# Rounding g behind its leaky step, another product order in the first batch, and another order at both ends of an attention + two-MoE kernel

## The chip, the cores and the metric

The kernel runs on one core of a Trainium2 chip. The metric is the device time of one execution in microseconds. The core has a matrix engine (TensorE, PE in the profile; its weight loads are PEld), VectorE (DVE), ScalarE (ACT), GpSimd (POOL), a sync engine (SP) that issues transfers, and 16 DMA engines. TensorE writes PSUM, which VectorE and ScalarE read; each engine works off its own queue in order.

## The reference, cut to what matters

```python
# q, k, v: (8, 8, 576, 64), phi: (8, 8, 576, 32)
a = exp(phi - max(phi, axis=2)); a = a / (sum(a, axis=2) + 1e-9)
k_m = einsum('bhsm,bhsd->bhmd', a, k); v_m = einsum('bhsm,bhsd->bhmd', a, v)
attn = softmax(q @ k_m^T / 8)            # over the 32 memory slots
x = (attn @ v_m), heads side by side     # (4608, 512)
h = x @ w_in; g = maximum(0.01 * h, h); x = g @ w_out                 # 512 -> 2048 -> 512
out = (sigmoid(x @ w_gate) * (x @ w_val)) @ w2_out                    # 512 -> 1536 -> 512
```

The inputs arrive as 64-bit floats and the output is 32-bit.

## The kernel before

The inputs are 64-bit numbers read as pairs of 32-bit words; ScalarE, VectorE and GpSimd turn each piece of a weight into a 32-bit float in steps called a, b, b2, c, d. A call of `tick` advances this pipeline by one piece. The wide products are made from numbers split into a rounded high part (a cast on ScalarE) and the rest (a subtraction on VectorE or GpSimd), three products for one: `split` does this.

**Stage one** goes over 8 batches of 576 tokens. A unit is (batch, group of 4 heads); its softmaxes run as a chain of small steps v1, t1, v2, ..., v11, where t steps are TensorE products and v steps work on the other engines. v_m is multiplied into w_in beforehand (`vw_block`, or `vw_pair` from batch 1 on), so that the hidden layer comes from the attention weights at_hi, at_lo directly. A loop step i stands for one half of a batch (288 tokens) and 128 of the 2048 hidden columns. `m1_in` makes the six hidden products into a bank of ps_h (two banks), Prelu (L861) puts the leaky result into grs, and the function that m1_in returns splits it into ghl (cast at L188, subtraction at L189). `m1_out` multiplies g into w_out: twelve products into four accumulators (L880); where a group of hidden columns ends, the accumulators are copied or added to obuf or pbuf (L887, L889). m1_in runs two steps ahead (LA = 2).

The order of the work is written out by hand. In step i of the loop (L1373 on) these are queued: the split of the g of step i + 1 (`fin`), the six products and the Prelu of step i + 2, the v steps of units due now together with ticks (or, later, the preparation of the second stage's weights, `stash`), the t steps, the v_m blocks, and last the output products of step i. The first batch (steps 0 to 31) runs while w_in and w_out are still being decoded; its order of halves is four hidden blocks for one half, four for the other. Ahead of the loop a prologue of groups (`SCHED['prologue']`) runs units (0,0) and (0,1); in a group the entries of one unit form a chain, T is a tick, and the chains take turns. Behind the prologue come v_m blocks 0 and 1 and m1_in for steps 0 and 1.

**Stage two** takes tokens in five pairs of blocks with seven products for eight, with the output products in `m2_out` (L1165), whose results VectorE adds into sums (L1175). In the last pair of 2 x 384 tokens the sums are turned by 32x32 transposes (L1147) into tiles called turned and stored (L1205): in chunks of 256 and 128 tokens, a transpose is put on a list (`lazy`) and runs behind later additions, and each store of four transfers goes out when all of the columns of one block of tokens are turned, in rows of 128 floats.

The lines in question:

```python
        gr = gr_next()
        nc.scalar.activation(gr, p[:, :HALF], AF.Prelu, alpha=0.01)
        gt[b, hf, fc] = (gh, gl)
        return lambda: split(gr, gh, gl, nc.vector if ... else nc.gpsimd)
```

Of the kernel before, what the change touches and what calls it, by code (L numbers as in the profile page):

```python
# [26 lines left out]
 'ticks': [1, 1, 1, 1, 2, 1, 1, 2, 0, 1, 0, 1, 1, 2, 0, 0, 0, 1, 1, 1, 1, 1, 0, 0, 1, 0, 0, 0, 0, 0],  # L27
 'banks': 9,
 'lopool': [0, 1, 2, 3, 4, 5, 6, 7, 8, 9, 10, 11, 12, 13, 14],
# [93 lines left out]
def tile_kernel(  # L123
# [13 lines left out]
    nc = tc.nc  # L137
# [274 lines left out]
    def ghl_next():  # L412
        n_g[1] += 1
        i = n_g[1] % 3
        return ghl[:, i, :], ghl[:, 3 + i, :]
# [426 lines left out]
    gt = {}  # L842
    acc = {}

    def m1_in(b, hf, fc):
        p = ps_h.tile([P, 512], F32, tag="h", name="ps_h")
        t = vw[b, fc * P // VB]
        o = (fc * P) % VB
        n = 0
        for g in range(NG):  # L850
            wh, wl = t[:, 0, g, o:o + P], t[:, 1, g, o:o + P]
            i = at[b, hf, g]
            ah, al = at_hi[:, i, :], at_lo[:, i, :]
            if fc == NF - 1:
                at_free.append(i)
            for w, x in ((wh, ah), (wl, ah), (wh, al)):
                nc.tensor.matmul(p[:, :HALF], w, x, start=(n == 0), stop=(n == 3 * NG - 1))  # L857
                n += 1
        gh, gl = ghl_next()
        gr = gr_next()  # L860
        nc.scalar.activation(gr, p[:, :HALF], AF.Prelu, alpha=0.01)  # L861
        gt[b, hf, fc] = (gh, gl)
        return lambda: split(gr, gh, gl, nc.vector if b == 0 and hf * NF + fc in SCHED["gldve"] else nc.gpsimd)
# [139 lines left out]
    def read(*todo, turns=0):  # L1003
        for op in todo:
            op()
        n_read[0] += 1
        for op in later.pop(n_read[0], []):
            op()
        for _ in range(turns):
            if lazy:  # L1010
                lazy.pop(0)()
# [129 lines left out]
    def m2_out(n, th, between):  # L1141
        t0, h = PAIRS[n]
        last = th == NTH - 1
        end = n + 1 == len(PAIRS)

        def turn(j, e, x, m, st):
            lazy.append(lambda: nc.vector.transpose(  # L1147
                st[:, 0:m // 32, j - j % 2 + e], sums[j][:, e, x:x + m].rearrange("p (b r) -> p b r", r=32),
            ))

        def stored(t, x, m, st):
            f = lazy.pop()
            lazy.append(lambda: (f(), store(t0 + t * h + x, m, st, end)))

        chunks = [(0, 256), (256, h - 256)]
        st = {}
        for k, e in OUT_SEQ:
            start = k in (0, 2, 3)
            b = banks[e if k in (0, 1, 4, 6) else 2 + e][:, :h]
            wt = w_at.pop(0)  # L1160
            w = wt.rearrange("p (j l f) -> p j l f", j=TH // 2, l=2)
            i = 0
            for j in range(TH // 2):
                for l, r in ((0, 0), (0, 1), (1, 0)):
                    nc.tensor.matmul(  # L1165
                        b, w[:, j, l, :], ops[j][k][:, r, :h], start=(start and i == 0), stop=(i == 5),
                        skip_group_check=not start,
                    )
                    i += 1
            w_load(wt)  # L1170
            o = sums[SUM_OF[k]][:, e, :h]
            if th == 0 and k in (0, 2, 1, 6):
                read(lambda: nc.scalar.copy(o, b), turns=1)
            else:
                read(lambda: nc.vector.tensor_add(o, b, o), turns=2 if end and last else 1)  # L1175
            for f in between.pop(0) if between else ():
                f()
            if last and end and (j := {5: 1, 4: 3, 3: 0, 6: 2}.get(k)) is not None:
                t = j % 2
                for x, m in chunks:  # L1180
                    if (t, x) not in st:
                        st[t, x] = turned()
                    turn(j, e, x, m, st[t, x])
                    if (k, e) in ((4, 1), (6, 1)):
                        stored(t, x, m, st[t, x])
            elif last and not end and (k, e) in ((4, 1), (6, 1)):
                t = k == 4
                for x, m in chunks:
                    o = turned()
                    for j in (t, t + 2):  # L1190
                        for e2 in range(2):
                            turn(j, e2, x, m, o)
                    stored(t, x, m, o)
        while last and end and lazy:
            lazy.pop(0)()

    n_st = [0]

    def turned():
        n_st[0] += 1  # L1200
        return stage2[n_st[0] % len(stage2)]

    def store(n0, m, o, end):
        for g in range(4):
            (nc.scalar if end and g % 2 else nc.sync).dma_start(  # L1205
                out=out[n0:n0 + m, P * g:P * g + P].rearrange("(b p) d -> p b d", p=32),
                in_=o[32 * g:32 * g + 32, 0:m // 32].rearrange("p b q r -> p b (q r)"),
            )


    with tc.manual_schedule():
# [84 lines left out]
        def step_in(b, hf, fc):  # L1296
            if (b, hf) == (0, 0):
                done_until(2 * (fc - fc % 2) + 4)
            return m1_in(b, hf, fc)
# [5 lines left out]
        def unit_parts(i):  # L1305
            vs, ts_, ls = [], [], []
            for u, u0 in U0.items():
                parts = [n for n, k in SCHED[{1: "chain1", 2: "chain2"}.get(u[0], "chain")].items() if k == i - u0]
                v = [PARTS[n](u) for n in parts if n[0] == "v"]
                if v:  # L1310
                    vs.append(chain(v))
                ts_ += [(PARTS[n], u) for n in parts if n[0] == "t"]
                ls += [
                    (PARTS[n], u) for n in parts
                    if n[0] == "l" and u not in units[:3]
                ]
            return vs, ts_, ls
# [6 lines left out]
            else:  # L1324
                (unit_phi, unit_kv, unit_q)["pkq".index(x[0])](units[int(x[1])])
        waiting = []
        n_vw = n_in = 0
        fin = None
        for group in SCHED["prologue"]:
            vs, ts_ = {}, []  # L1330
            for n, f in enumerate(waiting):
# [22 lines left out]
        while n_vw < 2:  # L1354
            run([first_vw(n_vw)()])
            n_vw += 1
        for i in range(LA):
            fin = step_in(*steps[i])
            if i + 1 < LA:
                fin()  # L1360

        early = {0: [(x_open, ())] + [(x_load, (0, c)) for c in range(KD)]}
        for n in range(8):
# [7 lines left out]
        first = m2_group(0, 0, 0, 0)  # L1371
        held = None
        for i, (b, hf, fc) in enumerate(steps):  # L1373
            if fin:
                fin()
                fin = None
            if i + LA < len(steps):
                fin = step_in(*steps[i + LA])
            else:
                if not tmps:  # L1380
                    tmp_open()
                next(first)
                next(first)
            vs, ts_, ls = unit_parts(i)
            if held:
                vs.insert(0, held())
                held = None
            if i < len(SCHED["ticks"]):
                vs.append(chain([tick() for _ in range(SCHED["ticks"][i])]))
                i0 = i + 1  # L1390
                if i0 == len(SCHED["ticks"]):
                    assert pos[0] >= n_start + 5
                    convs[0].load()
                    convs[1].load()
            else:
                run(vs)
                vs = [stash(i - i0 - 1)]
            run(vs)
            for f, u in ts_:
                f(u)  # L1400
            if i in VW_AT[0]:
                held = first_vw(VW_AT[0][i])
            for n in {b, b + 1} - {0}:
                if i in VW_AT.get(n, []):
                    vw_pair(n, 2 * VW_AT[n].index(i))
            m1_out(b, hf, fc)
            for f, u in ls:
                f(u)
            if b == B - 1:
                if i % NS == 0:  # L1410
                    assert i - i0 - 1 >= at_
                    p1.close()
                    p2.append(ctx.enter_context(tc.tile_pool(name="p2", bufs=2, reuse_waits="tile")))
                for f, n in early.get(i % NS, []):
                    f(*n)
# [3 lines left out]
        for n in range(len(PAIRS)):  # L1419
# [23 lines left out]
                        eng = nc.vector if len(todo) < 3 else nc.gpsimd  # L1443
                        between[-1] += [lambda o=o: x_hi(*o), lambda o=o, eng=eng: x_lo(*o, eng)]
            m2_out(n, NTH - 1, between)
            if n + 2 == len(PAIRS):
                for _ in range(2):
                    t = p2[0].tile([P, 2 * PC], F32, tag="xr", name="turned", bufs=7)
                    stage2.append(t.rearrange("p (b q r) -> p b q r", q=4, r=32))


# [28 lines left out]
```

## Time and profile before

| | us |
|---|---|
| three runs, median (lowest to highest) | 1563.75 (1563.34 to 1563.9) |
| the profiled execution | 1563.91 |
| its span, first to last instruction | 1562.1 |
| TensorE busy | 1513.7 (97%) |
| VectorE busy | 949.9 (61%) |
| ScalarE busy | 818.4 (52%) |
| GpSimd busy | 455.2 (29%) |

The span is stage one up to about 700 us and stage two behind it. Durations are read from the one profiled execution; the rest of its time, 1.8 us, lies around the span. In the rows below, `tile<-tiles` names what an instruction writes and reads, L is the line of the kernel, and what stands in brackets behind a row is how long the engine had been idle and what released it.

### The profile page before, as it was taken

To read this page: it belongs to the slowest core of one execution; us is meant where nothing else is said; L and a number is where in the kernel's file an instruction comes from. 1 tells how busy PE (TensorE), PEld (TensorE's weight loads), DVE (VectorE), ACT (ScalarE), POOL (GpSimd) and SP (SyncE) were. 2 spreads that over 40 slices of the span, in tenths; PEclk is the share of its full clock that TensorE was granted. 3 is DMA by queue.
4 is the path that set the end of the run, shared out by engine and by line. 5 is a ranking of instruction groups with operands and counts; after the bars stand their busy time and mean duration, and the time that the engine had idled before them with its cause. 6 is when DMAs were issued, how large, how long until landed. Compare 5 with 4: busy or idle time off the path is not lost.

```text
span 1562.1 us, 28982 instructions
## 1 busy us (share of the span) xinstructions
PE 1513.7 (97%) x10508; PEld 1357.9 (87%) x10508; DVE 949.9 (61%) x1732; ACT 818.4 (52%) x1846; POOL 455.2 (29%) x445
## 2 busy tenths in 40 slices
PE   5788999999999999999999999999999999999997
PEld 2677999999999999999999988888888888889997
DVE  6886555556655555522066665757666865668567
ACT  5885565666566565644444454534532544435432
POOL 2986364554545445533200030004000210003000
PEclk9999999999999999999999999999999999999999
DMA  9822664555556555411398887667866687668875
GB/s 303 294 54 59 166 178 135 179 153 167 167 167 188 153 177 160 128 53 60 100 320 261 246 236 248 194 193 216 274 195 193 189 247 234 194 193 235 295 250 156
DMA packets 278094, 297.11 MB, mean 190 GB/s; under 512 B 102080, under 2 KB 176320, under 8 KB 277952
## 3 DMA queue, kind: packets, MB, share of 16 engines
q1 hardware_dynamic: 276288, 294.47, 63.0%
q8 instruction: 84, 1.38, 0.4%
q10 hardware_dynamic: 1664, 0.79, 0.2%
q14 instruction: 58, 0.48, 0.1%
HBM read 243.27 MB, written 51.90 MB: 189 GB/s over the span
## 4 chain that ended last, share of the span: by engine, by line
PE 79%; DVE 4%; ACT 1%; POOL 1%; issue 1%; DMA 0%; DVEq 0%; SPq 0%; ACTq 0%; POOLq 0%
PE acc L880 21%; PE ps_y L1030 18%; PE oacc L1165 13%; PE ps_h L857 10%; PE ps_z L1030 9%; PE ps_x L1030 5%; PE ps_vw L827 2%; DVE op L1046 1%; DVE sum L1175 1%; PE ps_kv L593 1%; POOL xo L953 1%; DVE sg L1049 1%; PE ps_sc L668 0%; DVE sg L1055 0%; DVE tmp L1058 0%
## 5 line engine op out<-in xcount | busy, mean ns | idle before, releaser
L880 PE MATMUL acc<-ghl,wo 128*128 128x288 f32 x3072 | 461.4, 299 | 7.3 <-ACT obuf L889 2.6
L880 PEld LDWEIGHTS acc<-ghl,wo 128*128 128x128 f32 x3072 | 420.3, 188 | 32.8 <-issue 10.7
L1030 PE MATMUL ps_y<-xo,wt 128*128 128x512 f32 (+1 forms) x1440 | 328.8, 368 | 0.0
L189 POOL TENSOR_TENSOR ghl<-grs,ghl 128x288 fp32r<-128x288 f32 x250 | 217.7, 873 | 317.7 <-ACT ghl L188 239.7
L1030 PEld LDWEIGHTS ps_y<-xo,wt 128*128 128x128 f32 x1440 | 262.5, 188 | 36.1 <-ACT tmp L1061 2.0
L1165 PE MATMUL oacc<-op,wt 128*128 128x512 f32 (+1 forms) x1260 | 265.1, 369 | 1.4 <-DVE sum L1175 0.5
L1165 PEld LDWEIGHTS oacc<-op,wt 128*128 128x128 f32 x1260 | 228.3, 188 | 35.8 <-DVE sum L1175 4.5
L861 ACT ACTIVATE grs<-ps_h 128x288 f32<-128x288 f32 x256 | 105.4, 412 | 248.7 <-PE ps_h L857 227.0
L1061 ACT COPY tmp<-ps_y 128x512 f32<-128x512 f32 (+1 forms) x180 | 98.0, 544 | 256.8 <-PE ps_y L1030 256.7
L857 PE MATMUL ps_h<-at_hi,vw 128*128 128x288 f32 x1024 | 214.1, 297 | 3.6 <-ACT vw L188 2.7
L953 POOL TENSOR_TENSOR xo<-xr,xo 128x512 fp32r<-128x512 f32 (+1 forms) x28 | 39.4, 1436 | 598.0 <-ACT xo L949 598.0
L857 PEld LDWEIGHTS ps_h<-at_hi,vw 128*128 128x128 f32 x1024 | 166.2, 190 | 5.0 <-ACT vw L188 3.6
L1030 PE MATMUL ps_z<-xo,wt 128*128 128x512 f32 (+1 forms) x720 | 167.6, 367 | 0.3 <-POOL xo L953 0.3
L1175 DVE TENSOR_TENSOR sum<-oacc,sum 128x512 f32<-128x512 f32 (+1 forms) x170 | 106.5, 633 | 89.9 <-PE oacc L1165 89.1
L857 PE MATMUL ps_h<-at_lo,vw 128*128 128x288 f32 x512 | 151.8, 297 | 0.0
L1030 PEld LDWEIGHTS ps_z<-xo,wt 128*128 128x128 f32 x720 | 131.7, 188 | 17.5 <-POOL xo L953 0.7
L1058 DVE TENSOR_TENSOR tmp<-ps_x,tmp 128x512 f32<-128x512 f32 (+1 forms) x60 | 38.0, 633 | 177.8 <-PE ps_x L1030 177.8
L1042 ACT CAST op<-sg 128x512 fp32r<-128x512 f32 (+1 forms) x180 | 103.4, 579 | 76.3 <-DVE sg L1049 47.5
L188 ACT CAST ghl<-grs 128x288 fp32r<-128x288 f32 x256 | 111.7, 436 | 1.9
L1046 DVE TENSOR_TENSOR op<-sg,op 128x512 fp32r<-128x512 f32 (+1 forms) x180 | 111.9, 645 | 0.5
L857 PEld LDWEIGHTS ps_h<-at_lo,vw 128*128 128x128 f32 x512 | 97.2, 190 | 0.0
L839 DVE TENSOR_TENSOR vw<-ps_vw,vw 128x256 fp32r<-128x256 f32 x112 | 39.7, 416 | 81.8 <-ACT vw L837 81.8
(177 smaller groups left out, 1750.0 us busy)
## 6 DMA issues: line engine op xcount, KB each, us to landing
wt<-gvs SPq DMA_DIRECT2D x420, 256.0 KB, 3.0
wt<-w2s SPq DMA_DIRECT2D x210, 256.0 KB, 3.0
gvs<-hl SPq DMA_DIRECT2D x60, 256.0 KB, 2.6
x2s<-obuf SPq DMA_DIRECT2D x15, 576.0 KB, 3.4
win<-in_moe_w_in_dram SPq DMA_DIRECT2D x16, 512.0 KB, 9.7
wo_bits<-in_moe_w_out_dram SPq DMA_DIRECT2D x16, 512.0 KB, 10.5
q<-in_q_dram SPq DMA_DIRECT2D x224, 36.0 KB, 3.0
w2s<-hl SPq DMA_DIRECT2D x30, 256.0 KB, 2.4
```

What stands on the lines that cost most here:

```text
L188: nc.scalar.copy(hi, raw)
L189: eng.tensor_sub(lo, raw, f32(hi))
L857: nc.tensor.matmul(p[:, :HALF], w, x, start=(n == 0), stop=(n == 3 * NG - 1))
L861: nc.scalar.activation(gr, p[:, :HALF], AF.Prelu, alpha=0.01)
L880: nc.tensor.matmul(a[d][:, :HALF], w[:, d * P:(d + 1) * P], x, start=(open_ and n == 0), stop=(close and n == 2),)
L953: eng.tensor_sub(t[:, 1, :h], x_operand(n, k, a), f32(t[:, 0, :h]))
L1030: nc.tensor.matmul(bank, w[:, l, a, :], x[:, r, :h], start=(start and i == 0), stop=(i == 5), skip_group_check=not start,)
L1042: return lambda: nc.scalar.copy(ops[j][k][:, 0, :h], x)
L1046: return lambda: nc.vector.tensor_sub(t[:, 1, :h], x, f32(t[:, 0, :h]))
L1061: return lambda: nc.scalar.copy(d, x)
L1165: nc.tensor.matmul(b, w[:, j, l, :], ops[j][k][:, r, :h], start=(start and i == 0), stop=(i == 5), skip_group_check=not start,)
L1175: read(lambda: nc.vector.tensor_add(o, b, o), turns=2 if end and last else 1)
```

## The change

Four things are changed; no product is added or left out.

1. m1_in now ends with a split that the caller runs at once: cast and subtraction of g are queued directly behind Prelu in the same step, where they stood at the start of the next.
2. In the first batch, steps 0 to 23, the output products stand ahead of the unit products and the v_m blocks; in steps 3 and 7 they stand ahead of the v steps and ticks too, and with them the copies of the accumulators. From step 24 on they stay last.
3. At the start, v_m block 0 is queued within the last group of the prologue, its split (VectorE's subtraction included) between v10.1 and v10t.1; m1_in of steps 0 and 1 is made in two halves, first the three products of head group 0 for both steps, then those of group 1.
4. At the end, in the last pair, each transpose takes the 384 tokens at once and runs directly behind its addition; a store goes out for each half of the columns: 16 transfers as before, in four batches, in rows of 64 floats. They go through two tiles of their own, in the places of tiles that stage two has done with.

```diff
-              'v10t.0 t8b.1 T v8a.1', 'v11.0', 'v8b.1 v9.1 T', 'T T v9e.1 T v10.1 v10t.1 v11.1'],
+              'v10t.0 t8b.1 T v8a.1', 'v11.0', 'v8b.1 v9.1 T', 'T T v9e.1 T v10.1 v0.1 v10t.1 v11.1'],
...
-    def m1_in(b, hf, fc):
-        p = ps_h.tile([P, 512], F32, tag="h", name="ps_h")
+    def m1_in(b, hf, fc, begun=None, gs=range(NG)):
+        p = begun or ps_h.tile([P, 512], F32, tag="h", name="ps_h")
...
-        n = 0
-        for g in range(NG):
+        n = 3 * gs[0]
+        for g in gs:
...
+        if gs[-1] < NG - 1:
+            return p
...
-                read(lambda: nc.vector.tensor_add(o, b, o), turns=2 if end and last else 1)
+                read(lambda: nc.vector.tensor_add(o, b, o), turns=1)
...
-                for x, m in chunks:
-                    if (t, x) not in st:
-                        st[t, x] = turned()
-                    turn(j, e, x, m, st[t, x])
-                    if (k, e) in ((4, 1), (6, 1)):
-                        stored(t, x, m, st[t, x])
+                if t not in st:
+                    st[t] = gp.tile([P, 1536], F32, tag="at_hi" if t else "at_lo", name="turned", bufs=1)
+                    st[t] = st[t].rearrange("p (b q r) -> p b q r", q=4, r=32)
+                turn(j, e, 0, h, st[t])
+                lazy.pop()()
+                if e:
+                    f = 64 * (j // 2)
+                    for g in range(4):
+                        (nc.scalar if g % 2 else nc.sync).dma_start(
+                            out=out[t0 + t * h:t0 + t * h + h, P * g + f:P * g + f + 64].rearrange("(b p) d -> p b d", p=32),
+                            in_=st[t][32 * g:32 * g + 32, :, j - t:j - t + 2].rearrange("p b q r -> p b (q r)"),
+                        )
...
-        n_vw = n_in = 0
-        fin = None
+        n_vw = 1
+        PARTS["v0"] = lambda u: first_vw(0)()
...
+        begun = [m1_in(*steps[i], None, (0,)) for i in range(LA)]
         for i in range(LA):
-            fin = step_in(*steps[i])
-            if i + 1 < LA:
-                fin()
+            m1_in(*steps[i], begun[i], (1,))()
...
-            if fin:
-                fin()
-                fin = None
             if i + LA < len(steps):
-                fin = step_in(*steps[i + LA])
+                step_in(*steps[i + LA])()
...
+            n_out = 2 if b or i >= NS - LA * 4 else 0 if i in (BEGIN[1] - 1, 2 * BEGIN[1] - 1) else 1
+            if n_out == 0:
+                m1_out(b, hf, fc)
...
             run(vs)
+            if n_out == 1:
+                m1_out(b, hf, fc)
             for f, u in ts_:
                 f(u)
...
-            m1_out(b, hf, fc)
+            if n_out == 2:
+                m1_out(b, hf, fc)
```

## Rows read from the trace of the kernel before

**Rows 1.** The page's first part: busy time of each engine, share, instructions.

```profile
PE 1513.7 (97%) x10508; PEld 1357.9 (87%) x10508; DVE 949.9 (61%) x1732; ACT 818.4 (52%) x1846; POOL 455.2 (29%) x445
```

**Rows 2.** Busy time by stretch: stretch, length, five engines, granted clock, DMA share, GB/s.

```profile
45.55:53.27 7.72, 4.86 (x19) 4.54 (x19) 6.29 (x10) 5.14 (x12) 5.54 (x7) 1.00 1.08 338
53.27:84.50 31.23, 27.60 (x244) 23.77 (x243) 26.09 (x31) 29.52 (x63) 28.94 (x22) 0.95 0.75 231
84.50:119.20 34.70, 31.94 (x284) 28.85 (x284) 29.21 (x46) 26.99 (x60) 30.41 (x26) 1.00 0.17 34
119.20:140.20 21.00, 17.02 (x145) 13.66 (x142) 14.35 (x23) 12.42 (x27) 17.53 (x15) 1.00 0.37 80
...
163.00:210.00 47.00, 44.74 (x435) 41.96 (x434) 24.81 (x48) 26.30 (x70) 22.52 (x24) 1.00 0.52 147
210.00:1530.00 1320.00, 1316.68 (x8870) 1190.07 (x8859) 783.04 (x1430) 670.75 (x1516) 325.60 (x328) 1.00 0.65 195
```

**Rows 3.** Waits of TensorE, 48.3 to 110 us: total us, times, longest.

```profile
PE ps_h L857 <- ACT vw L188: 2.7, 1, 2.7
PE ps_vw L808 <- POOL win L250: 2.1, 2, 1.1
PE acc L880 <- ACT obuf L889: 1.8, 1, 1.8
PE ps_m L544 <- DVE dg L538: 1.4, 2, 1.0
```

**Rows 4.** Waits of TensorE, 110 to 210 us.

```profile
PE acc L880 <- ACT ghl L188: 2.5, 3, 1.4
PE acc L880 <- POOL ghl L189: 1.6, 2, 1.3
PE ps_sc L668 <- DVE vw L189: 1.2, 1, 1.2
PE ps_kvT L638 <- ACT e L623: 0.8, 1, 0.8
```

**Rows 5.** Timeline of GpSimd before the loop: start, us, engine, line, operation.

```profile
47.13 0.98 POOL L189 TENSOR_TENSOR at_lo<-grs,at_hi 128x288 fp32r<-128x288 f32 x1
48.07 1.27 POOL L189 TENSOR_TENSOR wo<-y,wo 128x512 fp32r<-128x512 f32 x1
```

**Rows 6.** Timeline of TensorE: first output products, and those after the longest late wait.

```profile
53.27 2.11 PE L880 MATMUL acc<-ghl,wo 128*128 128x288 f32 x12
...
195.38 1.85 PE L880 MATMUL acc<-ghl,wo 128*128 128x288 f32 x12 [1.42 <-ACT ghl L188]
```

**Rows 7.** Timeline of ScalarE: Prelu and what follows it, two places.

```profile
50.63 0.41 ACT L861 ACTIVATE grs<-ps_h 128x288 f32<-128x288 f32 x1 [1.90 <-PE ps_h L857]
51.07 0.43 ACT L188 CAST ghl<-grs 128x288 fp32r<-128x288 f32 x1
...
57.44 0.41 ACT L861 ACTIVATE grs<-ps_h 128x288 f32<-128x288 f32 x1
57.74 0.66 ACT L218 ACTIVATE y<-win 128x512 f32<-128x512 f32 x1
```

**Rows 8.** Timeline of the tail: stores on SP, VectorE's last addition and transposes.

```profile
1552.70 6.36 SPq L1205 DMA_DIRECT2D out_dram<-turned  x8
...
1554.75 0.52 DVE L1175 TENSOR_TENSOR sum<-oacc,sum 128x384 f32<-128x384 f32 x1
1555.19 1.14 DVE L1147 STREAM_TRANSPOSE turned<-sum 128x256 f32<-128x256 f32 x4
```

**Rows 9.** Busy time of two microseconds of the tail, columns as in rows 2.

```profile
1553.00:1554.00 1.00, 1.00 (x7) 0.78 (x5) 1.00 (x4) 0.00 (x0) 0.00 (x0) 1.00 0.39 91
...
1560.00:1561.00 1.00, 0.00 (x0) 0.00 (x0) 0.00 (x0) 0.00 (x0) 0.00 (x0) 0.50 0.40 112
```

**Rows 10.** ScalarE's DMA queue, 1545 to 1562.2 us: packets, MB, share of 16 engines.

```profile
q10 hardware_dynamic: 1664, 0.79, 19.5%
```

**Rows 11.** SP's DMA queue, 86 to 93 us, mostly q loads in rows of 128 B.

```profile
q1 hardware_dynamic: 3672, 0.45, 43.7%
```

More of the change, by code (lines that the diff above doesn't have):

```diff
@@ L1152, in stored @@
             f = lazy.pop()
-            lazy.append(lambda: (f(), store(t0 + t * h + x, m, st, end)))
+            lazy.append(lambda: (f(), store(t0 + t * h + x, m, st)))
         chunks = [(0, 256), (256, h - 256)]
@@ L1193, in m2_out @@
                     stored(t, x, m, o)
-        while last and end and lazy:
-            lazy.pop(0)()
     n_st = [0]
@@ L1201, in turned, with store @@
         return stage2[n_st[0] % len(stage2)]
-    def store(n0, m, o, end):
+    def store(n0, m, o):
         for g in range(4):
-            (nc.scalar if end and g % 2 else nc.sync).dma_start(
+            nc.sync.dma_start(
                 out=out[n0:n0 + m, P * g:P * g + P].rearrange("(b p) d -> p b d", p=32),
@@ L1445, in tile_kernel @@
             m2_out(n, NTH - 1, between)
[L1446 to L1449, printed above, removed]
 _INS = ['q', 'k', 'v', 'phi', 'moe_w_in', 'moe_w_out', 'moe2_w_gate', 'moe2_w_val', 'moe2_w_out']
```

## The prediction

> **What bounds the kernel now.** I read the busy table first: TensorE works 1513.7 us of the 1562.1 us span [rows 1], so a change that removes no product can at most win what is left: about 48 us of idle, and the stretches in which a product takes longer than elsewhere. The table by stretch says where that idle is [rows 2]: from 210 to 1530 us it is 3.3 us in 1320, from 163 to 210 us 2.3 us, and from 45.55 to 140.2 us 2.9 + 3.6 + 2.8 + 4.0 = 13.2 us. The rest lies before 45.55 us, where no product of the loop can run yet, and behind the last product. So three places count: the first batch, the stretch behind it, and the tail.
>
> In the same table the other engines are to be read beside TensorE. From 53.27 to 84.5 us ScalarE is busy 29.52 of 31.23 us; from 84.5 to 119.2 us GpSimd 30.41 of 34.70. There a TensorE wait is only the place where a late engine shows; taking the wait away does not make that engine faster. From 163 us on, neither is near full.
>
> The waits name what TensorE stood for: up to 110 us the rounded v_m block of the first loop step (2.7), decoded w_in for a v_m block (2.1), the copy of the closed accumulator to obuf (1.8) and the diagonal dg of a unit (1.4) [rows 3]; from 110 to 210 us the rounded g (2.5 on ScalarE, 1.6 on GpSimd), a PSUM buffer held by a v_m split (1.2) and the rounded e (0.8) [rows 4].
>
> **The change, part by part.** The sum is made against the profiled execution: span 1562.1 us, 1563.91 us in all, 0.16 us above the median of 1563.75 us. The same products run in every part; only order changes.
>
> *Start of the loop.* Before, the first L857 product waits 2.7 us, since the vw cast stands in ScalarE's queue behind all of the prologue [rows 3]. After, the cast of block 0 stands ahead of the last decode tick, and the g = 0 halves of steps 0 and 1 need only that. But their g = 1 halves need at_lo of unit (0,1), and here the new item in the round-robin moves it back: GpSimd's subtraction for at_lo (47.13 us, 0.98) stood ahead of a wo subtraction (48.07 us, 1.27) [rows 5]; one item more in the unit's chain puts wo first. ScalarE, with the vw cast of about 0.5 us put ahead, ends that wo cast near 47.6 us, so GpSimd's wo ends near 48.9 and at_lo near 49.7 instead of 48.1. Step 0 then ends near 50.0, step 1 near 50.7, step 2 near 52.1, and the first L880 group begins at 52.1 instead of 53.27 us [rows 6]: 1.1 us won. With the old order in GpSimd it would have been about 2.5; with a slower pace of the first products (they start after another gap) it can be 0.
>
> *53.27 to 84.5 us, ScalarE's stretch.* The obuf copies of steps 3 and 7 now stand ahead of the ticks, so the wait of 1.8 us goes, with the clock loss behind it: the granted clock is 0.95 of full speed over this stretch, a loss of 0.05 x 31.23 = 1.6 us [rows 2]. TensorE then runs into the next late thing: the third product group onwards needs a PSUM buffer of ps_h that Prelu has read, and Prelu stands in ScalarE's queue behind the ticks of the step before, now as before. ScalarE had 31.23 - 29.52 = 1.7 us of slack. Against it, Prelu and cast are now back to back and dependent: such a cast starts 0.44 us after its Prelu (50.63, 51.07), where an independent instruction follows after 0.30 (57.44, 57.74) [rows 7]. Against the usual pitch of 0.33 that is 0.11 us for each of about 10 steps, 1.1 us. Net 0.6 us. Bounds: 0 and the 5.2 us of TensorE's idle and clock loss.
>
> *84.5 to 119.2 us, GpSimd's stretch.* The output products, 1.6 us a step, now cover the wait for decoded w_in and for dg; the unit products come those 1.6 us later, but VectorE, which reads most of them, is itself busy 29.21 of 34.70 us there [rows 2] and comes to them late, so I cost that at nothing; were VectorE idle at that moment, it would wait up to 1.6 us, with the decode of that step queued behind it. GpSimd has 34.70 - 30.41 = 4.3 us of slack [rows 2], part of it because Prelu waits for the g subtraction and with it the ticks; with g a step earlier I take half, 2.0 us. Bounds 0 and 2.8, TensorE's own idle.
>
> *119.2 to 140.2 us.* The wait for g on GpSimd (its longest is 1.3) goes, since the subtraction is issued a step earlier; 1.2 for the PSUM buffer and 0.8 for e lie behind 1.6 us of output products [rows 4]. That is 3.3 of the 4.0 us idle; a v_m block that is split late stays late, and ScalarE and GpSimd are not moved by all of it: 2.5 us.
>
> *163 to 210 us.* Here the order of unit and output products is as before; only the cast moves. The longest wait, 1.42 us at 195.38 [rows 6], has ScalarE stuck behind a buffer of the weight preparation while the cast of that step's g is queued behind it. Directly behind Prelu it is done some 6 us earlier. What is late next is the next Prelu, and TensorE reaches that one a group of output products (1.6 us) later, so this wait goes; of the other 0.9 us I count half: 1.8 us. Bounds 0 and 2.3.
>
> *Beyond.* TensorE waits there so little [rows 2] that I count nothing: -1 to +1 us. SP's queue is not touched before the tail; the stores of x2s and the loads keep their places.
>
> *Tail.* Before, VectorE adds the last product at 1554.75 and then has four transposes, 1.14 us, before the last stores [rows 8]. The stores are 1.57 MB in two bursts: issued from 1552.70 us, the engines move data from 1553.6 (0.39 of that microsecond) to 1560.4 (0.40 of that one) [rows 9], and the span ends 1.7 us later. After, four batches of 393 KB leave at about 1549.8, 1551.75, 1553.7 and 1555.7 us, the last when its one transpose (half of 1.14) is done; data moves 0.9 us later. Each batch is 1536 rows of 256 B where there were rows of 512 B. One packet of 512 B took 0.195 x 16 x 17.2 us / 1664 = 32 ns [rows 10], and one of mostly 128 B, read, 0.437 x 16 x 7 us / 3672 = 13.3 ns [rows 11]. No row has a store of 256 B. On the line between the two it is 19.6 ns, a batch 96 x 19.6 = 1.9 us on 16 engines, just under the 1.96 us between batches: the last ends at 1556.6 + 1.9 = 1558.5, the span at 1560.2, 1.9 us won. Bounds: half of a 512 B packet (16 ns) gives 2.25 us won; the same 32 ns gives batches of 3.1 us, which queue from 1550.7 on: 1550.7 + 12.4 + 1.7 = 1564.8, 2.7 us lost; twice that is a rival below. I take 19.6 because the small packets of rows 11 show that the price falls with size.
>
> Sum: 1.1 + 0.6 + 2.0 + 2.5 + 1.8 + 1.9 = 9.9 us; 1563.9 - 9.9 = 1554.0 us.
>
> **The rivals.** *One: the decode is the bound.* If ScalarE and GpSimd keep their pace up to 140 us and take the freed waits back as waits for ps_h, the 6.2 us of the first batch shrink to 2: 1558.2 us. For it: the two fullest rows of the table; against: both have slack after 119 us. *Two: small stores cost as much each as large ones* (32 ns): the tail loses 2.7 instead of winning 1.9, 1558.6 us. *Three, the slow side: each 256 B store is worth two 512 B packets,* as when the place written is first read. At 64 ns a batch takes 6.2 us: 1550.7 + 24.7 + 1.7 = 1577.1, 15 us lost, 1570.9 us in all. The point from which the kernel gets slower is where four batches eat the other 8.0 us: (1570.1 - 1552.4) / 4 = 4.4 us a batch, 46 ns a packet. For it: nothing before stores so little at once; against: rows 11. *Four: nothing moves,* if the g = 1 wait, the ticks and the stores each give back what is won: about 1563.
>
> Three is what the Trainium skill's page DMA: Bandwidth & Descriptors gives in its section Specifications: below 512 B a transfer is read, modified and written. It gives no price for it, and no run here shows such a store yet; by that rule the change trades one long burst for four that each take longer.
>
> **How the numbers follow.** Forecast 0.60, one 0.18, two 0.12, three 0.06, four 0.04. A measurement of this kernel tells 0.2%, 3.1 us, from no change. Best case: GpSimd's whole idle in the first batch, 2.2 + 2.3 + 4.3 + 3.5 = 12.2, with 2.3 and 2.25: 1547. One and two together give 1562.8. The range 1548 to 1560.5 leaves out three, four and the ends. Faster: 0.59 of the forecast, 0.15 of one, 0.10 of two, 0.84; same 0.10, with four; slower 0.06, three.
>
> **What would show it.** Right: the g cast directly behind each Prelu; no L880 wait for obuf near 66 us; no wait at 195 us; first L880 group near 52 us; ScalarE over 95% busy from 52 to 83 us; the first batch done 6 us earlier; data of the stores from about 1543 us, each batch about 1.9 us. Wrong: ps_h waits of several us in the first batch (one); stores still in the engines well past the last transpose plus 3 us (two, three); the first L880 group 2.5 us earlier or not at all.

## The result and the profile after

The changed kernel takes 1576.62 us (median, 1574.52 to 1578.98) against 1563.34 us for the kernel before on the same chip (median of five runs, the three of the first table among them): ratio 1.0083 [1.0071, 1.0094], **13 us slower**. The prediction was 1554.0 us, faster; the time lies outside its range and none of its rivals names what happened. The profiled execution took 1574.52 us, its span 1572.7 us.

The busy table of after (busy us, share, instructions) is to be held against [rows 1]: the same number of TensorE instructions, and 20 us more of ScalarE (on which the last section).

```profile
PE 1517.0 (96%) x10508; PEld 1358.2 (86%) x10508; DVE 952.1 (61%) x1724; ACT 838.6 (53%) x1846; POOL 448.3 (29%) x445
```

Busy time by stretch, after (columns as in [rows 2]):

```profile
45.55:53.27 7.72, 6.48 (x23) 5.26 (x22) 6.70 (x11) 6.05 (x14) 6.34 (x8) 0.50 1.09 330
53.27:84.50 31.23, 26.35 (x242) 22.92 (x240) 26.80 (x30) 29.04 (x63) 27.30 (x21) 1.00 0.77 236
84.50:119.20 34.70, 31.35 (x245) 27.87 (x246) 30.66 (x45) 27.50 (x59) 29.81 (x26) 1.00 0.19 35
119.20:140.20 21.00, 17.20 (x160) 13.65 (x158) 12.71 (x20) 12.86 (x27) 15.46 (x13) 0.92 0.38 80
...
163.00:210.00 47.00, 45.27 (x407) 42.69 (x407) 24.73 (x49) 27.93 (x67) 21.22 (x22) 1.00 0.48 133
210.00:700.00 490.00, 480.36 (x4642) 447.27 (x4642) 264.64 (x534) 306.51 (x775) 235.51 (x254) 1.00 0.52 154
700.00:1530.00 830.00, 828.57 (x4196) 733.40 (x4196) 509.87 (x881) 375.66 (x733) 85.90 (x77) 1.00 0.71 216
```

and one stretch of before, which [rows 2] had inside a longer one:

```profile
210.00:700.00 490.00, 488.09 (x4696) 456.75 (x4685) 270.18 (x535) 296.23 (x785) 243.67 (x256) 1.00 0.53 154
```

**Read the row from 210 to 700 us.** TensorE was idle for 1.9 us there before, and is idle for 9.6 us after. This is the stretch that the prediction costed at nothing. Stage two (700 to 1530 us) is the same to 0.02 us. The first batch, where 6.2 us were to be won, has no more busy time than before: the four rows up to 140.2 us add up to 81.4 us in both kernels. The granted clock of 0.50 in the first row, where [rows 2] has 1.00, is not a loss: the first hidden products start 0.24 us apart in both kernels, at 49.43 and 49.67 us before, at 50.77 and 51.01 after (later, at 54.84 and 54.97 after, 0.13 us apart).

Landmarks say the same. Each half of a batch ends with a store of its accumulators (x2s, on SP); the second ends the first batch, the thirteenth comes 5.5 batches later. From the timelines of SP and TensorE:

| us | before | after |
|---|---|---|
| first output products | 53.27 | 52.60 |
| second x2s store | 163.25 | 164.96 |
| thirteenth x2s store | 651.48 | 662.95 |
| between these two | 488.2 | 498.0 |
| start of the last output products of stage two | 1538.37 | 1549.73 |
| from there to the span's end | 23.73 | 22.97 |

So the start won 0.7 us, the first batch gave that back and 1.7 more, the 5.5 batches behind it lost 9.8 us, and the tail won 0.8. Of the 9.8 us, 7.2 are idle time of TensorE (4.2 us between the two stores before, 11.4 after); the other 2.6 us are the same products taking longer in all (484.06 us busy before, 486.62 after), and no run shows why. These are landmarks of the two profiled executions, 10.6 us apart; that of after was the fastest of its runs, the medians are 13 us apart. The 0.7 us of the start is no more than executions differ by: in e4 below, whose start is that of before, the first output products come at 52.41 us.

**What TensorE waits for.** Waits of TensorE, 48.3 to 110 us, after (total us, times, longest):

```profile
PE ps_vw L808 <- POOL win L250: 4.3, 3, 2.8
PE acc L882 <- ACT pbuf L891: 1.8, 1, 1.8
PE ps_m L544 <- DVE dg L538: 1.1, 1, 1.1
PE ps_h L857 <- POOL at_lo L189: 1.0, 1, 1.0
```

The same list from 110 to 210 us, after:

```profile
PE ps_kvT L638 <- ACT e L623: 1.5, 1, 1.5
PE ps_h L857 <- ACT vw L188: 1.3, 1, 1.3
PE ps_h L857 <- ACT grs L863: 1.1, 2, 0.9
PE acc L882 <- POOL ghl L189: 0.8, 1, 0.8
```

The waits of [rows 3, 4] for obuf, for the rounded g on ScalarE and for the vw buffer are gone; in their place TensorE stands 2.2 us longer for decoded w_in, 1.8 us for the other copy of the accumulators, to pbuf (0.6 before), 1.3 us for a rounded v_m block, and longer for a step of the units (e). From 210 to 690 us, after:

```profile
PE ps_vw L827 <- DVE mx L535: 3.1, 3, 1.7
PE ps_kv L584 <- DVE t L575: 2.6, 4, 1.4
PE acc L882 <- ACT obuf L891: 2.0, 4, 0.8
PE ps_sc L668 <- ACT kvT L650: 1.5, 1, 1.5
```

and before:

```profile
PE ps_sc L668 <- ACT kvT L650: 0.8, 1, 0.8
PE acc L880 <- ACT obuf L889: 0.7, 2, 0.4
PE ps_kv L584 <- DVE t L575: 0.3, 1, 0.3
```

None of these is for g, whose rounding was moved. Three are for small steps of the units (mx, t, kvT), the fourth for a copy of the accumulators. And GpSimd's own waits for the cast of g, L189 behind L188, grew in these 480 us; before, then after:

```profile
POOL ghl L189 <- ACT ghl L188: 160.9, 67, 5.7
```

```profile
POOL ghl L189 <- ACT ghl L188: 213.1, 101, 4.3
```

**One step followed through.** The t1 product of a unit (TensorE, L530) runs at 228.41 us before and at 229.96 after, so here after is 1.55 us behind. Before, GpSimd and ScalarE, two timelines:

```profile
226.10 1.75 POOL L250 TENSOR_TENSOR y<-y,k 128x512 int32<-128x512 int32 x1
227.80 0.81 POOL L189 TENSOR_TENSOR ghl<-grs,ghl 128x288 fp32r<-128x288 f32 x1
228.56 1.17 POOL L730 TENSOR_TENSOR e<-e,st 128x576 f32<-128x576 f32 x1
```

```profile
226.28 0.41 ACT L861 ACTIVATE grs<-ps_h 128x288 f32<-128x288 f32 x1 [1.09 <-PE ps_h L857]
226.59 0.66 ACT L228 ACTIVATE k<-raw 128x512 f32<-128x512 uint32 x1
227.15 0.43 ACT L188 CAST ghl<-grs 128x288 fp32r<-128x288 f32 x1
```

The cast stands behind a piece of decode, and GpSimd has finished its own decode (y) when the subtraction comes up; it starts without a wait. After, GpSimd, then ScalarE (two places), VectorE and TensorE:

```profile
228.84 0.82 POOL L189 TENSOR_TENSOR ghl<-grs,ghl 128x288 fp32r<-128x288 f32 x1 [2.29 <-ACT ghl L188]
229.60 1.29 POOL L250 TENSOR_TENSOR y<-y,k 128x512 int32<-128x512 int32 x1
231.23 0.80 POOL L189 TENSOR_TENSOR ghl<-grs,ghl 128x288 fp32r<-128x288 f32 x1 [0.33 <-POOL y L250]
231.99 1.16 POOL L730 TENSOR_TENSOR e<-e,st 128x576 f32<-128x576 f32 x1
```

```profile
228.62 0.67 ACT L228 ACTIVATE k<-raw 128x512 f32<-128x512 uint32 x1
...
233.18 0.68 ACT L741 ACTIVATE e<-e 128x576 f32<-128x576 f32 x1 [2.08 <-POOL e L730]
```

```profile
233.89 0.75 DVE L747 TENSOR_REDUCE st<-e 128x18 f32<-128x576 f32 x1 [5.80 <-ACT e L741]
```

```profile
234.90 1.09 PE L827 MATMUL ps_vw<-win,kvT 64*32 64x256 f32 x30 [1.74 <-DVE mx L535]
```

GpSimd stands for 2.29 us before a subtraction whose cast isn't done, its decode (y) queues behind it, and the unit's e behind the decode and one more subtraction. e's last input, the maximum st, is made by VectorE; before, then after:

```profile
224.77 0.74 DVE L723 TENSOR_REDUCE st<-e 128x18 f32<-128x576 f32 x1
```

```profile
226.75 0.74 DVE L723 TENSOR_REDUCE st<-e 128x18 f32<-128x576 f32 x1
```

After, st is done at 227.49 us and e starts at 231.99. The decode has less to lose by the 2.29 us: its k, which ScalarE makes behind Prelu and cast, is done at 229.29, and it starts at 229.60. e comes 231.99 - 228.56 - 1.55 = 1.88 us late against TensorE's own position; 226.75 - 224.77 - 1.55 = 0.43 of that are already in st, the rest is GpSimd's queue. The exponential waits for e, VectorE's sum waits for the exponential, the maximum mx is queued behind that sum, and TensorE waits 1.74 us for mx.

### The profile page after: what moved, and what is told of

Same layout as the page of the kernel before. It is cut to its first block, busy times and chain, and to the rows that moved or that the text cites. A ratio compares the mean times of both kernels' runs of the same rounds, so it can differ in the third digit from the quotient of the medians.

```text
span 1572.7 us, 28931 instructions
## 1 busy us (share of the span) xinstructions
PE 1517.0 (96%) x10508; PEld 1358.2 (86%) x10508; DVE 952.1 (61%) x1724; ACT 838.6 (53%) x1846; POOL 448.3 (29%) x445
## 4 chain that ended last, share of the span: by engine, by line
PE 75%; DVE 5%; ACT 2%; issue 1%; POOL 1%; DMA 1%; SPq 0%; ACTq 0%; DVEq 0%; POOLq 0%
PE acc L882 18%; PE ps_y L1032 18%; PE oacc L1167 13%; PE ps_z L1032 9%; PE ps_h L857 9%; PE ps_x L1032 5%; PE ps_vw L827 1%; DVE op L1048 1%; DVE sum L1177 1%; PE ps_kv L593 1%; POOL xo L955 1%; DVE sg L1051 1%; DMA gvs<-sums 1%; PE ps_sc L668 0%; DVE sg L1057 0%
## 5 line engine op out<-in xcount | busy, mean ns | idle before, releaser
L189 POOL TENSOR_TENSOR ghl<-grs,ghl 128x288 fp32r<-128x288 f32 x250 | 215.1, 861 | 351.6 <-ACT ghl L188 309.3
L188 ACT CAST ghl<-grs 128x288 fp32r<-128x288 f32 x256 | 110.8, 433 | 8.1
L1032 PE MATMUL ps_x<-xo,wt 128*128 128x512 f32 (+1 forms) x360 | 83.7, 367 | 0.0
```

The costliest lines, as they stand in the source:

```text
L188: nc.scalar.copy(hi, raw)
L189: eng.tensor_sub(lo, raw, f32(hi))
L1032: nc.tensor.matmul(bank, w[:, l, a, :], x[:, r, :h], start=(start and i == 0), stop=(i == 5), skip_group_check=not start,)
```

## The experiments

Two theories came out of this reading; both are about what is queued *behind* the moved instructions, not about g. **H, GpSimd:** the subtraction, queued in the step in which its Prelu runs, stands at the head of GpSimd's queue before its input exists, and the units' and the decode's work waits behind it. **R, ScalarE:** at its old place the cast filled the time in which ScalarE waits for TensorE's hidden products; behind Prelu it delays the units' ScalarE work. Rivals: the order of the first batch (part 2), the start (3) or the tail (4) costs the time, or a buffer of g is held longer. "Batches" below is the time between the second and the thirteenth x2s store, 488.2 us before.

| | median us | ratio [interval] | second x2s | batches | PE busy 210 to 700 |
|---|---|---|---|---|---|
| after | 1576.62 | 1.0083 [1.0071, 1.0094] | 164.96 | 498.0 | 480.36 |
| e1 | 1567.8 | 1.0029 [1.0018, 1.004] | 163.95 | 491.7 | 484.16 |
| e2 | 1561.5 | 0.9991 [0.9981, 1.0] | 161.65 | 487.2 | 488.56 |
| e3 | 1581.79 | 1.012 [1.0101, 1.0139] | 171.32 | 498.2 | 480.08 |
| e9 | 1572.66 | 1.0057 [1.004, 1.0073] | 167.23 | 494.25 | 483.97 |
| e11 | 1573.63 | 1.0062 [1.0047, 1.0077] | 166.35 | 492.1 | 485.50 |
| e12 | 1570.66 | 1.0044 [1.0028, 1.0061] | 162.57 | 497.0 | 481.51 |
| e14 | 1564.15 | 1.0003 [0.9994, 1.0012] | 165.30 | 487.0 | 488.68 |

Landmarks come from one execution each and can differ by 1.6 us between executions in parts that nothing touched (the thirteenth store is at 651.48 us before and at 649.83 in e4, which changes the tail alone); medians carry the verdicts.

**Part 1 undone (e2).** Everything else of the change stays.

```diff
...
-                step_in(*steps[i + LA])()
+            if fin:
+                fin()
+                fin = None
+            if i + LA < len(steps):
+                fin = step_in(*steps[i + LA])
```

> The changed kernel with part 1 undone alone: cast and subtraction at the start of the next step as before, all else of the change kept. H and R both: 1560 to 1565 us. Rival S (part 1 is harmless; the new start and the order of the first batch shift the units against the loop, and that costs later): stays at 1574 to 1577 us.

1561.5 us: the other three parts together are worth -2.1 us (interval -0.2% to 0), and the batches are as before. The whole loss is in part 1, or in part 1 together with the others.

**Part 1 alone (e3)**, on the kernel before.

```diff
-            if fin:
-                fin()
-                fin = None
             if i + LA < len(steps):
-                fin = step_in(*steps[i + LA])
+                step_in(*steps[i + LA])()
```

> The kernel before with part 1 alone: cast and subtraction directly behind Prelu, nothing else changed. H and R: 1572 to 1577 us, with TensorE idle about 11 us from 210 to 700 us. S: 1561 to 1564 us.

1581.79 us, 18.2 us slower than before and 4.8 above what H and R gave, with the same 10 us in the batches as after and 8.1 us in the first batch. Waits of TensorE in e3, 48.3 to 163 us, the first two:

```profile
PE ps_vw L808 <- POOL win L250: 5.4, 4, 2.8
PE ps_kvT L638 <- ACT e L623: 3.6, 1, 3.6
```

It is the decode and the units that come late, as in after. So the other parts aren't guilty; with part 1 they take 5.2 us of its cost back, of which they win 2.1 without it too (e2). By the second x2s store (171.32 in e3, 164.96 in after) that is in the first batch; that output products ahead of late unit products cover them there fits this, but wasn't tried by itself.

**Cast early, subtraction at its old place (e1)**, on the changed kernel: this parts H from R.

```diff
-        return lambda: split(gr, gh, gl, nc.vector if ... else nc.gpsimd)
+        eng = nc.vector if ... else nc.gpsimd
+        nc.scalar.copy(gh, gr)
+        return lambda: eng.tensor_sub(gl, gr, f32(gh))
```

and the caller as in e2.

> The changed kernel, with the cast of g still directly behind Prelu, but the subtraction (GpSimd, a few on VectorE) queued at the start of the next step, where it was before. Theory H (GpSimd's queue: the subtraction of a g that TensorE has just made stands ahead of the step's other GpSimd work, which waits about 2 us each step): the loss of some 10 us behind 210 us goes, 1562 to 1567 us, TensorE's idle from 210 to 700 us back from about 11 to about 3 us. Rival R (ScalarE's queue: the cast ahead of the units' work is what delays them): 1574 to 1577 us, idle unchanged.

1567.8 us, between the two, 0.8 us above what H gave. Of the 15.1 us from e2 to after, the cast's place is 1567.8 - 1561.5 = 6.3 us and the subtraction's place, with the cast already moved, 1576.6 - 1567.8 = 8.8 us. Both theories hold, neither alone.

**A needless copy behind each Prelu (e9, e11)**, on e2: g's split stays at its old place, and ScalarE has one more instruction of 224 columns at the place where part 1 puts the cast. In e9 it copies within the bank of ps_h, in e11 within a tile of its own. The copies are not used.

```diff
         nc.scalar.activation(gr, p[:, :HALF], AF.Prelu, alpha=0.01)
+        nc.scalar.copy(p[:, HALF:512], p[:, 0:512 - HALF])   # e9
+        nc.scalar.copy(scr, scr)                             # e11
```

> The changed kernel with part 1 undone, and one needless copy of 224 columns (about 0.3 us) on ScalarE behind each Prelu; the cast and the subtraction stand where they stood before. Theory R (ScalarE had cast g in the time in which it waits for TensorE anyway; behind Prelu any 0.3 to 0.45 us delays the units' work of that step, and the units have little slack): most of the 6.3 us by which the early cast alone is slower, 1565 to 1568 us. Rival (the early cast costs by its wait on the Prelu just before it, or by its own data, not by its place): 1561 to 1563 us.

> The kernel that has all of the change but part 1 (e2_split_late, 1561.5 us), with a needless copy of 224 two-byte columns of a tile of its own on ScalarE directly behind each Prelu. The copy's results are not used; what is computed stays the same. No bank of PSUM is held longer by it, as the copy of e9_extra_copy (1572.7) did hold ps_h. Theory R (anything on ScalarE between Prelu and the units' work makes the units' chains later, since from 140 us on their slack against TensorE is smaller than such an instruction): 1565 to 1572 us, TensorE's busy time from 210 to 700 us 482 to 486 of 490 us. Rival (the loss of e9 came from the bank of ps_h held longer, and with it the loss of the early cast is not explained by its place): 1561 to 1563 us, busy 488.

1572.66 and 1573.63 us: 11.2 and 12.1 us over e2, and 4.7 and 1.6 us above what R gave. The two losses don't lie in the same places. At the thirteenth store e9 is 12.6 us behind e2, e11 9.5 us. Another 4.9 us of e11's profiled execution lie behind that store, in stage two, where no copy stands: its 128x512 products into ps_y and ps_z took 392 ns each on average, in every other kernel here 389, and no run shows why. So e11, which holds no bank longer, still loses 9.5 us where its copies are; a held bank isn't needed for the loss, though up to 3 us of e9's may come from it.

Both lose more than the 6.3 us of the cast. They add work where the cast is work moved, and the copy was not tried at another place in the step, so that the place by itself costs rests on e1 and on e14 below. What these two show is that an engine with idle time doesn't take an instruction for nothing: ScalarE is busy for only 296.8 of 490 us in e2.

**Subtraction later still (e12)**, on e2, from the second batch on: the cast at the start of the step, the subtraction behind the step's other GpSimd work.

```diff
-                fin()
+                low = fin()          # cast now, returns the subtraction
...
             run(vs)
+            if low:
+                low()
```

> The kernel of e2_split_late with, from the second batch on, the subtraction of g moved the other way: the cast stays at the start of the step, the subtraction is queued on GpSimd behind the step's other GpSimd work. Theory H (GpSimd works in order, and a subtraction queued before its cast is done holds up the units' copies and subtractions behind it): the units gain what little GpSimd wait is left, 1560 to 1562 us, and GpSimd's waits for the cast of g from 210 to 690 us fall from about 160 us to below 100. Rival (the place of the subtraction matters only through the output products, which need it): late means TensorE waits for the rounded g, 1564 to 1570 us, with waits of the output products for GpSimd in the list.

1570.66 us, 0.7 above what the rival gave: H's expectation failed in this direction and the rival's mechanism holds. GpSimd's waits for the cast fell only to 130.1 us, and the output products now wait for the subtraction. Waits of TensorE in e12, 210 to 690 us, the first two:

```profile
PE acc L888 <- POOL ghl L869: 6.4, 7, 2.0
PE ps_vw L827 <- DVE vw L839: 0.9, 1, 0.9
```

6.4 us of the 7.1 us that TensorE is idle beyond e2. There was no unit wait to win in e2, so fewer GpSimd waits were worth nothing; GpSimd's wait time by itself is no measure of loss.

**Prelu, cast and subtraction together behind the step's unit work (e14)**, on the changed kernel, from the second batch on. The split is still made in the same step as the hidden products, a step earlier than before; only what stands behind it differs.

```diff
-                step_in(*steps[i + LA])()
+                fin = step_in(*steps[i + LA])     # Prelu and split are in fin
+                if b == 0:
+                    fin()
+                    fin = None
...
             run(vs)
+            if fin:
+                fin()
```

> The changed kernel with, from the second batch on, Prelu, cast and subtraction moved together behind the step's unit work, still in the step of the hidden products. Both theories (H, subtraction ahead of the units' GpSimd work; R, cast ahead of the units' ScalarE work) say that the units then wait for nothing new: of the 10 to 11 us lost from 163 to 650 us most comes back, 1564 to 1567 us in all, with the second store of x2s near 165 us and the thirteenth near 653. Rival (the loss comes from the split being in the same step at all, as by grs or ghl buffers held longer, whatever stands behind it): 1572 to 1577 us, as the changed kernel. A third way: Prelu late holds the banks of ps_h, and TensorE waits for those: over 1567 us with ps_h waits in the list.

1564.15 us: 12.5 of after's 13.3 us come back. The batches take 487.0 us, as in e2; what is left is the first batch, which stays as in after. The step followed above, in e14 (its t1 product at 231.24 us, 2.83 behind before), GpSimd and then TensorE:

```profile
231.74 1.17 POOL L730 TENSOR_TENSOR e<-e,st 128x576 f32<-128x576 f32 x1
```

```profile
234.67 1.09 PE L827 MATMUL ps_vw<-win,kvT 64*32 64x256 f32 x30 [0.22 <-DVE mx L535]
```

e is 231.74 - 228.56 - 2.83 = 0.35 us late instead of 1.88, and the wait is 0.22 us instead of 1.74. And GpSimd still waits 180.9 us for casts from 210 to 690 us, but the units' work of the step now stands ahead of the subtraction. So it is the place in the queues that costs, not the earlier step, nor buffers of g held longer.

**Part 2 alone (e5)**, the order of the first batch on the kernel before.

```diff
+            n_out = 2 if b or i >= NS - LA * 4 else 0 if i in (3, 7) else 1
+            if n_out == 0:
+                m1_out(b, hf, fc)
...
             run(vs)
+            if n_out == 1:
+                m1_out(b, hf, fc)
...
-            m1_out(b, hf, fc)
+            if n_out == 2:
+                m1_out(b, hf, fc)
```

> The kernel before with the new place of the output products in the first batch alone. Start and order together moved the end of the first batch by 1.6 us (second x2s store at 161.65 where it was 163.25 us, with part 1 undone). If the order carries it: 1561.5 to 1562.5 us and that store near 161.7 us. If it is the start, the order is worth nothing by itself since ScalarE and GpSimd keep their pace: 1563 to 1564 us, store at 163.2 us. The prediction's own terms would give 5 us: 1558.5 us.

1563.39 us, ratio 1.0 [0.9991, 1.001]: nothing. The second x2s store, expected at 161.7 or 163.2 us, came at 165.04 in the profiled execution, which was the slowest of the ten (1565.35 us). The waits it was to cover are gone, and another has their place. Waits of TensorE in e5, 48.3 to 163 us:

```profile
PE acc L880 <- POOL ghl L189: 8.3, 6, 2.3
PE ps_h L857 <- ACT vw L188: 2.8, 1, 2.8
PE ps_vw L808 <- POOL win L250: 0.3, 1, 0.3
```

Output products that run earlier need g earlier, and g comes from GpSimd, whose pace nobody changed: the mechanism of the prediction's rival One (freed waits taken back), with a wait for g where it named ps_h.

**The two ends (e4 tail, e6 start, e10 start with another turn, e13 both ends).** e4, e6 and e13 put parts 4, 3, and both on the kernel before; e10 is e2 with block 0's split and its neighbour in the same turn of the prologue, so that at_lo keeps its place on GpSimd:

```diff
-        PARTS["v0"] = lambda u: first_vw(0)()
+        PARTS["v0"] = v0        # runs first_vw(0) whole, takes no turn
```

> The kernel before with the new tail alone (one transpose a sum, four batches of stores in rows of 256 B). From the change's own trace, where the tail from the first L1167 product to the end took 0.75 us less: 1562.6 us (1562.0 to 1563.2). If the tail's price had been the reason, 1570 or more.

> The kernel before with the new start alone (v_m block 0 in the last prologue group, m1_in of steps 0 and 1 in halves). By the prediction 1.1 us: 1562.5 us, first output products near 52.2 us, with a wait for at_lo of about 1 us before step 0's last product. If what is won there is given back to the engines behind: 1563 to 1564 us.

> The changed kernel with part 1 undone, and v_m block 0 split in the turn of v10t.1 instead of a turn of its own, so that GpSimd's at_lo of unit (0,1) stands ahead of wo again. If that place cost the front: the wait for at_lo (1.0 us) goes, first output products about 1 us earlier, 1560.5 to 1561 us; if ScalarE and GpSimd set the pace behind, 1561.5 us as with the turn of its own.

> The kernel before with parts 3 and 4 alone (start and tail), parts 1 and 2 left as they were. Alone they measured 1562.89 and 1562.70 us against 1563.6. If they add: 1562.0 us (1561 to 1563), and the order of part 2 is worth what e2_split_late (1561.5) has over this, at most 1 us. If the start's gain is taken back before the tail: 1562.7.

e4 1562.7 us (0.9994 [0.9984, 1.0003]), e6 1562.89 (0.9996 [0.9987, 1.0006]), e13 1562.05 (0.9993 [0.9984, 1.0003]), e10 1562.42 (0.9993 [0.9983, 1.0002]). e4, e6 and e13 came out within 0.4 us of what was expected, e10 at neither of its two values. By medians the ends add: -0.9, -0.8, together -1.6 us; none by itself can be told from no change. In e10 the wait for at_lo (1.0) is gone and the total is no better than e2: a TensorE that is earlier in the first batch waits for g there (8.8 us from 48.3 to 163 us, in e2 8.3). No version here beats the kernel before by more than can be told: e2, the best, is 2.1 us under it.

## Why the prediction was wrong

**The failed step: "with g a step earlier", counted as pure gain.** In the stretch from 84.5 us it took half of GpSimd's slack as won, from 119.2 us it wrote that the wait for g goes "since the subtraction is issued a step earlier", and beyond 210 us it counted nothing. Each time it asked who *waits for* g and not what is *queued behind* its subtraction and cast. A subtraction issued earlier than its input can be there doesn't run earlier; it holds the queue. In the trace of before both facts could be seen: GpSimd's 160.9 us of waits for the cast, already at the old place, and the 159 us in which Prelu waited for TensorE from 210 to 690 us, a wait ahead of which the cast stood at its old place, and behind which part 1 put it. The Trainium skill's page Perfetto Trace Analysis, section Tensor Engine Instruction, says that ScalarE, VectorE and GpSimd work strictly in order; the trace agrees: the unit's e, whose input was done at 227.49 us, started at 231.99, behind the subtractions.

**The second failed step: "Beyond" costed at nothing because TensorE hardly waits there.** 1.9 us of idle in 490 says that every feeder arrives just in time; it doesn't say by how much. The e of a unit made 1.88 us later cost 1.74 us of TensorE: slack of about 0.1 us in that step. A stretch at 99.6% has nothing to win and much to lose; the term, with bounds of -1 and +1 us, measured -9.9 from the third store to the thirteenth. The reading of the table "From 163 us on, neither is near full" (ScalarE 296 of 490 us, GpSimd 244, in the row of before from 210 to 700 us) was true and didn't matter.

By terms:
- *Start, 1.1 us.* The path was right: TensorE waits 0.98 us for at_lo, up to 49.88, and the first output products come at 52.60 instead of 52.1. 0.67 won in the trace, 0.8 by medians (e6), neither more than the runs differ by; the first output products lie at 52.41 to 53.27 us in the four kernels with the old start. The loss of the wo turn was right too, but e10 shows that without it nothing more is won.
- *53.27 to 84.5 us, 0.6.* The obuf wait is gone, as said, but at 81.82 us TensorE waits as long, 1.81 us, for the copy to pbuf. The granted clock of this stretch rose from 0.95 to 1.00, but that of the stretch from 119.2 us fell from 1.00 to 0.92. The 0.11 us for a cast that depends on its Prelu was the wrong price: it left out the wait of what stands behind, w_in's decode, 4.3 us of TensorE waits where [rows 3] had 2.1.
- *84.5 to 140.2 us, 4.5.* The order alone is worth nothing (e5): covered waits come back as waits for g. With part 1 those waits are gone and the unit waits take their place.
- *163 to 210 us, 1.8.* The wait at 195 us is gone, as said; TensorE's busy time there rose by 0.5 us of the 2.3 idle, since other waits came in; from the second store to the third, 0.15 us was won.
- *Beyond, 0.* -9.9 us from the third store to the thirteenth.
- *Tail, 1.9.* 0.8 to 0.9 us won (from the last output products to the span's end 22.84 to 23.11 us in the ten kernels with the new tail, 23.73 to 23.88 in the four with the old). The packets were priced right; VectorE wasn't.

**The tail's rows.** ScalarE's DMA queue in after, 1545 to 1572.7 us (packets, MB, share of 16 engines):

```profile
q10 hardware_dynamic: 3200, 0.79, 14.3%
```

0.143 x 16 x 27.7 us / 3200 = 19.8 ns a packet of 256 B, where 19.6 was taken from the line between two other sizes. So rivals Two (32 ns) and Three (64 ns) are false. Busy time by microsecond, after:

```profile
1563.00:1564.00 1.00, 1.00 (x8) 1.00 (x7) 0.97 (x3) 0.00 (x0) 0.00 (x0) 1.00 0.89 175
...
1566.00:1567.00 1.00, 0.00 (x0) 0.00 (x0) 0.97 (x3) 0.00 (x0) 0.00 (x0) 1.00 0.92 196
...
1570.00:1571.00 1.00, 0.00 (x0) 0.00 (x0) 0.00 (x0) 0.00 (x0) 0.00 (x0) 0.50 1.01 212
```

Data of the stores ends just behind 1571 us, 1.7 us before the span, as predicted. But TensorE has ended and VectorE still works. VectorE's last steps, after:

```profile
1565.98 0.52 DVE L1177 TENSOR_TENSOR sum<-oacc,sum 128x384 f32<-128x384 f32 x1
1566.53 0.58 DVE L1149 STREAM_TRANSPOSE turned<-sum 128x384 f32<-128x384 f32 x1
1567.03 0.52 DVE L1177 TENSOR_TENSOR sum<-oacc,sum 128x384 f32<-128x384 f32 x1
1567.59 0.58 DVE L1149 STREAM_TRANSPOSE turned<-sum 128x384 f32<-128x384 f32 x1
```

An addition and a transpose of 384 tokens take 1.05 us a step, where before (additions of [rows 8], 1553.77 and 1554.75) a step took 0.98 us. Counted from the start of the last output products, the last addition came at 16.4 us before and comes at 17.3 after, the last transpose ends at 18.4 where the prediction had 17.3. That 1.1 us is what the tail's term lacked: the transposes taken off the end were put in front of the last addition, and VectorE had no room for them. It was full there before the change too, 1.00 of the microsecond in the first row of [rows 9].

## What to carry to other kernels

Before moving an instruction forward in an in-order queue, ask when its input is there and name what stands behind it: an early place is a gain only if the input is ready by then, and an idle engine is no cover. In a stretch where the bound engine is at 99% or more, every feeder may be just in time; cost a moved instruction there by its own length, and the wait for its input, on the feeders' chains, from zero down, and look for the place behind the urgent work (e14) or in the engine's own wait (the old place).

## What the runs showed of the hardware that was not expected

Stores of 256 B rows cost 19.8 ns a packet against 32 ns for 512 B [rows 10]: a quarter more per byte, not twice, at 175 to 212 GB/s in the three rows above. The Trainium skill's page DMA: Bandwidth & Descriptors, section Specifications, says that below 512 B a transfer is read, modified and written. The section gives no price for it; the rows here are dearer by a quarter, and none of them shows whether a read stands behind that.

ScalarE's busy time is 20 us higher in every kernel in which the cast follows its own Prelu (after 838.6, e1 839.1, e3 838.5, e14 838.0) and not in those with the cast at its old place and no copy added (before 818.4, e2 819.1). No instruction was added: 20.2 us / 256 = 0.08 us for each g. The rows fit that: a cast that needs the result of the Prelu ahead of it starts 0.44 us behind it, when the Prelu of 0.41 us has ended, an independent instruction 0.30 us behind it, while it still runs [rows 7]. e14 has these 20 us and beats after by 12.5: busy time in itself was not the loss.
